# An attention and routed-experts kernel: weight chunks fetched one group later, one-hot rows and first split exchanged on GpSimd, the single-block scale on VectorE, a left-over half in front of a branch

## The chip, the cores and the metric

The kernel runs on one core of a Trainium2 chip. The metric is the time of one execution on the device in microseconds (us), lower is better. The engines of the core have a queue each and meet at semaphores: TensorE (PE; its weight loads are PEld), VectorE (DVE), ScalarE (ACT), GpSimd (POOL) and SyncE (SP), which issues most of the DMAs. A "q" behind an engine's name (ACTq) means its sequencer: branches, register loads and semaphore waits.

## The reference: what is computed

First attention over 4 batches of 8 heads, 768 positions of 64 numbers. Each query sees the keys less than 16 positions away, and 24 summaries, one for each block of 32 positions (the maximum of the keys, the mean of the values, with log 32 added to the score). The output, 3072 rows of 512 numbers, goes into a layer of eight experts with sticky routing:

```python
for s in range(S):
    fresh_e = int(np.argmax(logits[b, s]))
    if s == 0 or local_gate[b, s] < 0.5:
        e = fresh_e
    else:
        e = prev_e if prev_e >= 0 else fresh_e
    ...
    h = np.maximum(x[b, s] @ w1[e], 0.0)
    out[b, s] = p[e] * (h @ w2[e])
```

Here p is the softmax of the row's logits, w1 is 512 x 1024 and w2 is 1024 x 512 for each expert.

## The kernel before, in words

**Attention.** The 32 heads are 16 pairs (4 batches of 4 pairs), and each pair is done in two groups of 384 positions, so there are 32 groups, G = 0 to 31; pair n = G // 2. The loop over G in `attention` writes the instructions of all engines in one fixed order, and each engine runs its own in that order. In group G stand: `s_mm(G)`, the scores (L305 puts in the mask, L311 multiplies queries by the key windows kb); `t_stage(G - 2)`, transposes of the probabilities (L337, copied by ScalarE in L338); `s_max(G)` on VectorE (L319, the row maximum nm) and `s_exp(G)` on ScalarE (L327, six exponentials); `a_mm(G - 3)`, the value products (L348); `a_norm` on VectorE (L359, L360). Between them stand small steps of the routing of an earlier batch, which the method `small` lets in by counts of groups, and the transposes and logits of finished rows (L553, L570). One routing step, L640 on VectorE, writes sc, and the matmuls L644 to L647 on TensorE read it, in front of `a_mm(G - 3)` of group 26.

GpSimd prepares the next pair. In the first group of pair n come `windows(n + 1)` (L269, the keys' windows, scaled, into kb) and `fold_v(n + 1)` (L254, adds halves of the value blocks of vt into vf); in the second group `summaries(n + 1)` (L272, the block maxima ks, which VectorE computes in L243, into the last columns of kb) and `spread_v(n)` (L283, copies of the value means into vw). The scores of pair n + 1 cannot start before L272.

SyncE loads keys (kp, L197), queries (q, L206), values transposed (vt, L202) and value windows (vw, L210) some pairs ahead, and stores finished rows (L365), all through one queue.

**Jobs that ride along.** `tick(G, point)` runs jobs that were put at a group. Once the first batch is routed, the expert with the most rows of it, e0, is known, and `have_e0` places fetches and splits of e0's weights. A chunk is 128 x 1024 numbers, 512 KB: `wfetch` loads one into a buffer wst (four buffers, L1146), `wsplit` turns it into a high and a low part, ScalarE casting the high part (L1150), and GpSimd (four pieces, L1158) or VectorE (L1153) subtracting. The tables say at which G:

```python
SET0 = 25
WFETCH = (21, 21, 22, 22, 26, 30)
WSPLIT = (24, 29)
```

The same file has at point 1 of group SET0 the one-hot rows of the first batch, `self.set0()`: six GpSimd instructions (L682) that write A. In group G the order at the end is: GpSimd's windows and folds or summaries and copies, the loads, `tick(G, 1)`, `set0` if G is SET0.

**Experts.** Rows are sorted by expert into blocks of 128 and computed in calls of three, two or one blocks. `blocks` computes the first layer and all but one of the second-layer halves; the last half of each call is left to `left_over`, which runs in front of the next call and in which the next call's weights are split, under a branch that a flag (`words`) decides (`splits`, L1513). How many calls there are of each size depends on the data; every engine branches on a register: L1646 for calls of three, L1650 of two, L1662 of one. A single-block call is `single`: eight first-layer products in two halves, eight second-layer products, then `store`, which scales the result by the routing weight (psort) out of PSUM into yo, on ScalarE (L1205) where its third argument is true, on VectorE (L1208) otherwise, and scatters it to the output from GpSimd (L1209). After `store` the method loads two flags on ScalarE, VectorE and GpSimd and branches on them.

The end of the program reads so before:

```python
with tc.If(n1 > 0) as some:
    emit(self.left_over(AT1, splits(0, LANE3, 2), splits(1, LANE3)))
    call1(0)
    ...
with some.Else():
    emit(self.left_over(AT1))
```

With the data of these runs one call of one block is executed.

Of the kernel before, what the change touches and what calls it, by code (L numbers as in the profile page):

```python
# [35 lines left out]
CALL = 3  # L36
N3, N2, N1, MORE, SURE = 8, 8, 8, 2, 3
# [5 lines left out]
AT1 = AT2 + 2 + 2 * (N2 + MORE)  # L43
SLOTS = AT1 + 2 + N1 + MORE
LANE1, LANE2 = N3 + MORE, N3 + MORE + 1
LANE3 = LANE2 + N2 + MORE
# [4 lines left out]
WARM = 11  # L51
WHOLE = (3, 4, 5)
LATE = (*WHOLE, 9, 13)
SET0 = 25
BEHIND = (5, 16, 24, 30)
SOON = (8, 12)
FILL = {2: 5}

WFETCH = (21, 21, 22, 22, 26, 30)
WSPLIT = (24, 29)  # L60
WBY = "GGGVVVGV"

TAIL = {0: ("t", 30), 1: ("a", 29), 2: ("t", 31), 4: ("a", 30), 5: ("a", 31)}
# [21 lines left out]
class Kernel:  # L85
# [87 lines left out]
    def attention(self, tick, rows, tail):  # L173
        nc, tc, ident = self.nc, self.tc, self.ident
        with ExitStack() as ctx:
# [200 lines left out]
            for G in range(last_g):  # L376
# [84 lines left out]
                tick(G, 1)  # L461
                if G == SET0:
                    self.set0()
# [824 lines left out]
    def single(self, i, mid, w1, w2, refill):  # L1288

        nc = self.nc  # L1290
        hs = [self.mw.tile([P, 512], F32, name=f"hs{f}") for f in range(2)]

        def mm1(f, ks):
            for k in ks:
                if k == 0:
                    self.hp = self.bank("s")
                w = [x[0].rearrange("p (q k c) -> p q k c", k=KT, c=2 * P)[:, 2 * f:2 * f + 2, k] for x in (self.hi, self.lo)]
                self.mm(self.hp.rearrange("p (q c) -> p q c", q=2), self.xT[:, k, 0, 0], self.xT[:, k, 1, 0], w, k == 0, k == KT - 1)
                if k == KT - 1:
                    nc.scalar.activation(out=hs[f], in_=self.hp, func=AF.Relu)  # L1300

        mm1(0, range(KT))
        mm1(1, (0, 1))
        hT = [self.th(hs[0], 0), None]
        mm1(1, (2, 3))
        for w in range(2):
            refill(w, self.last_mm)
        yp = self.bank("a")

        def mm2(ks):  # L1310
            for k in ks:
                h, l = [x[:, P * (k % 4):P * (k % 4) + P] for x in hT[k // 4]]
                self.mm(yp, h, l, [x[1][:, k * DM:k * DM + DM] for x in (self.hi, self.lo)], k == 0, k == FT - 1)

        mm2((0, 1))
        hT[1] = self.th(hs[1], 1)
        mm2((2, 3))
        mid(0)
        mm2(range(4, 8))
        self.store(yp, i, True)  # L1320
        w1(0, 1, 2, 3)
        w2(0, 1, 2, 3)

# [53 lines left out]
    def run(self):  # L1377
        nc, tc = self.nc, self.tc
# [4 lines left out]
        def at(G, point, f, *args):  # L1383
            jobs.setdefault((G, point), []).append((f, args))
# [6 lines left out]
        def wfetch(j):  # L1391
            w, q = divmod(j, NCH)
            st["w", j] = self.awk.tile([P, CH], F32, name="wst", bufs=4)
            self.fetch(st["w", j], w, q * CH, (q + 1) * CH, st["e0"])

        def wsplit(j):
            w, q = divmod(j, NCH)
            self.split(w, q * CH, (q + 1) * CH, st.pop(("w", j)), nc.vector if WBY[j] == "V" else nc.gpsimd)

        def have_e0():  # L1400
            st["e0"] = nc.values_load(self.e0[0:1, 0:1], engines=(ENG.SP,), min_val=0, max_val=E - 1)
            for j in range(len(WSPLIT)):
                at(WSPLIT[j], 1, wsplit, j)
            for j in range(len(WFETCH)):
                at(WFETCH[j], 1, wfetch, j)

# [50 lines left out]
        def tail(stage):  # L1457
# [3 lines left out]
            for k in range(XL[-1] + 4):  # L1461
# [5 lines left out]
                if k in WLAST:  # L1467
                    wsplit(len(WSPLIT) + WLAST.index(k))
                if k in WLATE:
                    wfetch(len(WFETCH) + WLATE.index(k))  # L1470
                for u in range(NU):
# [8 lines left out]
        def reg(i, engines, hi):  # L1480
            return nc.values_load(self.words[0:1, i:i + 1], engines=engines, min_val=0, max_val=hi)  # L1481
# [7 lines left out]
        def split(w, chunks, by=None):  # L1489
            for q in chunks:  # L1490
                eng = nc.vector if SPLIT_BY[by or w][q] == "V" else nc.gpsimd
                self.split(w, q * CH, q * CH + CH, st["stage"][w][:, q * CH:q * CH + CH], eng)

        def have_all():
            while "words" not in st:
                self.small(1, True)

        def splits(w, lane, by=None):
            new = []

            def weights(*chunks):
                if lane is None:
                    return
                if lane == LANE1:
                    split(w, chunks)
                    if chunks[-1] == NCH - 1:
                        st["spent"].append(w)
                        refills()
                    return
                if not new:  # L1510
                    have_all()
                    new.append(reg(lane, (ENG.Activation, ENG.DVE, ENG.Pool), 1))
                with tc.If(new[0] > 0):  # L1513
                    split(w, chunks, by or (2 if w and lane else None))

            return weights

        def late(lane):
            r = []

            def weights(w, after):
                have_all()
                if not r:
                    r.extend((reg(2 * LANES + lane, (ENG.SP,), 1), reg(LANES + lane, (ENG.SP,), E - 1)))
                with tc.If(r[0] > 0):
                    refill(w, r[1], after)

            return weights

        def calls(n, blocks, lane):  # L1530

            def mid(half):
                if half < blocks:
                    while n < AT2 and st["next"] <= n + half:
                        self.small(1, True)
                    self.tx(n + half, half)
                    if n < AT2:
                        freed()
                    elif n + half + blocks < (AT1, SLOTS)[n >= AT1]:
                        self.gather(n + half + blocks)  # L1540

            return mid, splits(0, lane), splits(1, lane)
# [9 lines left out]
        with ExitStack() as ctx:  # L1552
# [10 lines left out]
            def refills():  # L1563
                if "words" in st:
                    while st["spent"]:
                        refill(st["spent"].pop(0), st["words"])
# [24 lines left out]
            def emit(*what):  # L1591
                for _ in chain(*what):
                    pass
# [51 lines left out]
            n3, n2, n1 = st["ends"]  # L1645
# [9 lines left out]
            def call1(n):  # L1655
                i = AT1 + 2 + n
                self.single(i, *calls(i + 1, 1, LANE3 + n + 1), late(LANE3 + n))

            with tc.If(n1 > 0) as some:
                emit(self.left_over(AT1, splits(0, LANE3, 2), splits(1, LANE3)))  # L1660
                call1(0)
                with ExitStack() as c:  # L1662
                    for n in range(1, N1):
                        c.enter_context(tc.If(n1 > CALL * n))
                        call1(n)
            with some.Else():
                emit(self.left_over(AT1))


def tile_kernel(tc, *args):  # L1670
# [90 lines left out]
```

## Time and profile before

| what | us |
|---|---|
| median of 3 runs | 436.49 |
| lowest and highest run | 434.3, 437.31 |
| the profiled execution | 433.81 |
| its span, first to last instruction | 432.0 |
| TensorE busy in the span | 416.2 |
| VectorE busy | 234.1 |
| ScalarE busy | 197.5 |
| GpSimd busy | 165.9 |

The profile is that of one execution. Start times count from the start of the span. A busy share is an average over stages that differ: attention fills the first 125 us or so, and the experts the rest. TensorE's matmuls are pipelined and their ends modelled, so a busy TensorE may still be one that waits a little; where it is listed with an idle time, it surely did.

### The profile page before, as it was taken

How to read it: one execution, taken by the hardware profiler on the slowest of the kernel's cores; microseconds unless marked ns; L12 is line 12 of the kernel's file. 1: busy time of each engine (PE TensorE's matmuls, PEld its weight loads, DVE VectorE, ACT ScalarE, POOL GpSimd, SP SyncE). 2: the span in 40 equal slices, each digit the busy share in tenths (PEclk: the TensorE clock that was granted, in tenths of full speed). 3: DMA queues.
4: the chain of work that ended last, by engine and by line, in shares of the span. 5: the costliest groups of instructions: out<-in, count | busy, mean ns of one | idle time of the engine just before them, and what ended most of it. 6: DMA issues, size and time to landing. Idle time of an engine off the chain costs nothing.

```text
span 432.0 us, 11296 instructions
## 1 busy us (share of the span) xinstructions
PE 416.2 (96%) x4227; PEld 360.3 (83%) x4228; DVE 234.1 (54%) x575; ACT 197.5 (46%) x466; POOL 165.9 (38%) x255
## 2 busy tenths in 40 slices
PE   7999999989999999999999999999999999999992
PEld 4787887868898798988987998799899889879781
DVE  4876796978788689957721022112435202254560
ACT  4988887967865227322121222122634212263561
POOL 3667686798624315753022103110630310321131
PEclk9999999989999999999999999999999999999997
DMA  8999999997251850394076912110257210219312
GB/s 310 403 396 402 400 329 377 401 402 284 95 177 68 325 212 0 99 368 170 2 284 231 374 52 72 29 50 0 99 185 255 90 58 0 57 53 388 105 51 58
DMA packets 22279, 83.27 MB, mean 193 GB/s; under 512 B 2702, under 2 KB 3344, under 8 KB 19120
## 3 DMA queue, kind: packets, MB, share of 16 engines
q1 hardware_dynamic: 17600, 67.75, 41.1%
q0 software_dynamic: 4448, 14.29, 10.0%
q8 instruction: 39, 0.64, 0.6%
q14 instruction: 48, 0.39, 0.3%
q10 hardware_dynamic: 144, 0.20, 0.2%
HBM read 69.65 MB, written 12.71 MB: 191 GB/s over the span
## 4 chain that ended last, share of the span: by engine, by line
issue 25%; DMA 12%; POOLq 5%; POOL 4%; PE 3%; DVE 3%; DVEq 0%
DMA out_dram<-yo,sidx 9%; POOLq L1273 4%; POOL xg L1164 2%; DMA out_dram<-few_y,sidx 2%; DMA xg<-x_dram,gidx 1%; DVE bp L1084 1%; POOL l L1158 1%; POOLq L1481 1%; PE bs L1249 1%; PE bt L1111 1%; PE bs L1251 0%; PE bs L1252 0%; DVE hT L1258 0%; DVE eqp L1078 0%; POOL out_dram L1209 0%
## 5 line engine op out<-in xcount | busy, mean ns | idle before, releaser
L1249 PE MATMUL bs<-xT,h 128*128 128x384 f32 (+1 forms) x288 | 91.3, 317 | 0.0
L1251 PE MATMUL bs<-xT,h 128*128 128x384 f32 (+1 forms) x288 | 89.8, 312 | 0.0
L1252 PE MATMUL bs<-xT,l 128*128 128x384 f32 (+1 forms) x288 | 89.7, 311 | 0.0
L1196 PE MATMUL ba<-h,hT 128*128 128x512 f32 x192 | 78.9, 411 | 1.4 <-PEq L1646 0.8
L1258 DVE SCALAR_TENSOR_TENSOR hT<-bs,hT 128x384 fp32r<-128x384 f32 (+1 forms) x56 | 33.2, 593 | 82.9 <-ACT hT L1256 69.2
L1198 PE MATMUL ba<-h,hT 128*128 128x512 f32 x192 | 75.3, 392 | 0.0
L1197 PE MATMUL ba<-l,hT 128*128 128x512 f32 x192 | 75.0, 391 | 0.0
L1256 ACT ACTIVATE hT<-bs 128x384 fp32r<-128x384 f32 (+1 forms) x56 | 29.3, 523 | 86.9 <-PE bs L1252 84.9
L1164 POOL DMA_INDIRECT xg<-x_dram,gidx x30 | 29.4, 981 | 101.5 <-PE bt L1175 90.5
L1249 PEld LDWEIGHTS bs<-xT,h 128*128 128x128 f32 x288 | 54.5, 189 | 0.8 <-issue 0.4
L327 ACT ACTIVATE pr<-bs,nm 128x120 f32<-128x120 f32 x192 | 51.7, 372 | 7.5 <-DVE nm L319 6.9
L1251 PEld LDWEIGHTS bs<-xT,h 128*128 128x128 f32 x288 | 54.5, 189 | 0.4
L1252 PEld LDWEIGHTS bs<-xT,l 128*128 128x128 f32 x288 | 54.5, 189 | 0.0
L1209 POOL DMA_INDIRECT out_dram<-yo,sidx x24 | 28.0, 1168 | 64.4 <-ACT yo L1205 40.9
L1196 PEld LDWEIGHTS ba<-h,hT 128*128 128x128 f32 x192 | 36.2, 189 | 8.7 <-issue 2.6
L1198 PEld LDWEIGHTS ba<-h,hT 128*128 128x128 f32 x192 | 36.0, 188 | 8.2
L1197 PEld LDWEIGHTS ba<-l,hT 128*128 128x128 f32 x192 | 36.2, 189 | 6.0
L1153 DVE TENSOR_TENSOR l<-stg,h 128x1024 fp32r<-128x1024 f32 x28 | 34.4, 1274 | 12.0 <-ACT h L1150 11.9
L1170 DVE TENSOR_TENSOR xT<-bt,xT 128x512 fp32r<-128x512 f32 x27 | 18.6, 691 | 36.5 <-ACT xT L1168 34.3
L1150 ACT CAST h<-stg 128x1024 fp32r<-128x1024 f32 x32 | 32.2, 1049 | 11.4 <-PEq L1646 4.6
L1205 ACT ACTIVATE yo<-ba,psort 128x512 f32<-128x512 f32 x24 | 16.5, 688 | 45.1 <-PE ba L1198 41.5
L283 POOL COPY vw<-vs 24x384 f32<-24x384 f32 x64 | 29.9, 509 | 13.6 <-ACT vs L278 5.4
(269 smaller groups left out, 639.4 us busy)
## 6 DMA issues: line engine op xcount, KB each, us to landing
stg<-in_w SPq DMA_DIRECT2D x16, 1024.0 KB, 7.7
vw<-in_vW SPq DMA_DIRECT2D x16, 780.0 KB, 7.4
few_w<-in_w SPq DMA_DIRECT2D x8, 1024.0 KB, 8.4
kp<-in_kT SPq DMA_DIRECT2D x16, 384.0 KB, 6.9
q<-in_qT SPq DMA_DIRECT2D x16, 384.0 KB, 7.6
vt<-in_vT SPq DMA_DIRECT2D x16, 384.0 KB, 7.0
x_dram<-xs SPq DMA_DIRECT2D x8, 768.0 KB, 5.8
wst<-in_w SPq DMA_DIRECT2D x8, 512.0 KB, 7.4
```

What stands on the lines that cost most here:

```text
L283: nc.gpsimd.tensor_copy(out=vw[n % 3][WL:W, t:t + NW // 4, :, 0:D], in_=vs.to_broadcast([NB, NW // 4, 2, D]))
L327: nc.scalar.activation(out=pr[:, h, u, 0:W], in_=sp[:, h, u, :], func=AF.Exp, bias=nm[:, h, u:u + 1], scale=1.0)
L1150: self.nc.scalar.copy(out=hi, in_=src)
L1153: eng.tensor_tensor(out=lo, in0=src, in1=hi.bitcast(F32), op=ALU.subtract)
L1164: self.nc.gpsimd.indirect_dma_start(out=t, out_offset=None, in_=rows, in_offset=bass.IndirectOffsetOnAxis(ap=self.gidx[:, i:i + 1], axis=0))
L1196: nc.tensor.matmul(out=ps, lhsT=ah, rhs=wh, start=first, stop=False)
L1197: nc.tensor.matmul(out=ps, lhsT=ah, rhs=wl, start=False, stop=False)
L1198: self.last_mm = nc.tensor.matmul(out=ps, lhsT=al, rhs=wh, start=False, stop=last).ins
L1249: ins = nc.tensor.matmul(out=ps[:, j], lhsT=wh, rhs=xh[c], start=(c == 0), stop=False).ins
L1251: nc.tensor.matmul(out=ps[:, j], lhsT=wh, rhs=xl[c], start=False, stop=False)
L1252: nc.tensor.matmul(out=ps[:, j], lhsT=wl, rhs=xh[c], start=False, stop=(c == KT - 1))
L1258: nc.vector.scalar_tensor_tensor(out=l, in0=ps, scalar=0.0, in1=h.bitcast(F32), op0=ALU.max, op1=ALU.subtract)
```

## The change

Five edits. The tables: the one-hot rows go from group 25 to group 24; the first four fetches of weight chunks from groups 21 and 22 to 22 and 23; the first split from group 24 to 25. In `single`, the store's scale goes from ScalarE to VectorE. At the end, `left_over` stands once, in front of the branch on n1, and the branch has no other side.

```diff
-SET0 = 25
+SET0 = 24
...
-WFETCH = (21, 21, 22, 22, 26, 30)
-WSPLIT = (24, 29)
+WFETCH = (22, 22, 23, 23, 26, 30)
+WSPLIT = (25, 29)
...
-        self.store(yp, i, True)
+        self.store(yp, i)
...
-            with tc.If(n1 > 0) as some:
-                emit(self.left_over(AT1, splits(0, LANE3, 2), splits(1, LANE3)))
-                call1(0)
-                with ExitStack() as c:
-                    for n in range(1, N1):
-                        c.enter_context(tc.If(n1 > CALL * n))
-                        call1(n)
-            with some.Else():
-                emit(self.left_over(AT1))
+            emit(self.left_over(AT1, splits(0, LANE3, 2), splits(1, LANE3)))
+            with ExitStack() as c:
+                for n in range(N1):
+                    c.enter_context(tc.If(n1 > CALL * n))
+                    call1(n)
```

On GpSimd, at the end of group 24 and through group 25 (l_122 and h_120 are the low and high parts of w1, wst a fetched chunk, A the one-hot rows, kb_139 the key windows of pair 13, vw_147 the value windows of pair 12):

```order
 L269 TENSOR_SCALAR kb_139<-kp_146 128x4x96 x3
 L254 TENSOR_TENSOR vf<-vt 128x192 x2
+L682 TENSOR_SCALAR A<-c_84,lanf 128x128 x6
+L272 TENSOR_SCALAR kb_139<-ks 128x12x24
+L283 COPY vw_147<-vs 24x6x64 x4
 L1158 TENSOR_TENSOR l_122<-wst,h_120 128x256 x4
-L272 TENSOR_SCALAR kb_139<-ks 128x12x24
-L283 COPY vw_147<-vs 24x6x64 x4
-L682 TENSOR_SCALAR A<-c_84,lanf 128x128 x6
 L269 TENSOR_SCALAR kb_138<-kp_145 128x4x96 x3
```

The split moves from in front of the summaries and copies to behind them, and the one-hot rows from behind the copies to in front of the summaries.

On SyncE, at the end of group 21 (kp_146 and q_136 are the keys and queries of pair 13, vt its values, vw_147 the value windows of pair 12; the ISA rows compute the address of a chunk):

```order
 L197 DMA kp_146<-in_kT 128x768
 L206 DMA q_136<-in_qT 128x768
-L1146 ISA
-L1146 DMA wst<-in_w 128x1024
-L1146 ISA
-L1146 DMA wst<-in_w 128x1024
 L202 DMA vt<-in_vT 128x768
 L210 DMA vw_147<-in_vW 128x1560
```

The first two chunks no longer stand in front of vt and vw; they come behind vw, and the next two behind the keys and queries of pair 14.

On VectorE, in the first single-block call (hT and xT are the low parts of transposed rows, yo the scaled result, words the flags):

```order
+L1660 COMPARE_AND_BRANCH
 L1170 TENSOR_TENSOR hT<-bt,hT 128x512
 L1525 UNCONDITIONAL_BRANCH x2
 L1170 TENSOR_TENSOR hT<-bt,hT 128x512
 L1170 TENSOR_TENSOR xT<-bt,xT 128x4x128
+L1208 TENSOR_SCALAR yo<-ba,psort 128x512
 L1481 TENSOR_LOAD words
 L1513 COMPARE_AND_BRANCH
```

The scale is new in VectorE's queue, in front of the loads of the flags; on ScalarE the same place loses L1205. The branch on n1, L1660 now, stands directly in front of the call.

## Rows read from the trace of the kernel before

**Rows 1.** Two stretches: busy us of each engine (instructions), granted clock, DMA share, GB/s.

```profile
92.05:95.46 3.41, 3.41 (x36) 3.00 (x34) 2.08 (x7) 2.81 (x9) 3.31 (x7) 0.51 1.02 397
95.55:104.15 8.60, 8.60 (x175) 7.35 (x178) 8.24 (x19) 6.73 (x23) 7.82 (x16) 1.00 0.90 334
```

**Rows 2.** Timeline of TensorE: start, duration, instruction, idle before it and what ended that.

```profile
88.25 0.35 PE L305 MATMUL bs<-me 64*64 64x360 bf16 x4
90.48 0.85 PE L311 MATMUL bs<-kb,q 64*64 64x120 f32 x24 [1.88 <-POOL kb L272]
91.26 0.87 PE L337 MATMUL bt<-ident,pr 128*124 128x128 f32 x6
91.96 0.17 PE L644 MATMUL bt<-sc,cb 128*128 128x8 bf16 x1
...
95.52 0.35 PE L305 MATMUL bs<-me 64*64 64x360 bf16 x4
...
99.15 0.35 PE L305 MATMUL bs<-me 64*64 64x360 bf16 x4
```

**Rows 3.** Timeline of GpSimd, groups 24 to 27.

```profile
84.85 1.15 POOL L254 TENSOR_TENSOR vf<-vt 128x192 f32<-128x192 f32 x2 [2.06 <-DMA vt<-in_vT]
87.25 2.78 POOL L1158 TENSOR_TENSOR l<-wst,h 128x256 fp32r<-128x256 f32 x4 [1.25 <-ACT h L1150]
89.99 0.43 POOL L272 TENSOR_SCALAR kb<-ks 128x288 f32<-128x288 f32 x1
90.49 1.85 POOL L283 COPY vw<-vs 24x384 f32<-24x384 f32 x4
92.44 3.52 POOL L682 TENSOR_SCALAR A<-c,lanf 128x128 bf16<-128x128 f32 x6
95.94 1.47 POOL L269 TENSOR_SCALAR kb<-kp 128x384 f32<-128x384 f32 x3
97.38 1.15 POOL L254 TENSOR_TENSOR vf<-vt 128x192 f32<-128x192 f32 x2
```

**Rows 4.** Timeline of VectorE in the same groups.

```profile
85.39 0.94 DVE L243 TENSOR_REDUCE ks<-kp 128x24 f32<-128x768 f32 x1
...
88.36 0.20 DVE L359 RECIPROCAL dn<-ba 128x6 f32<-128x6 f32 x1 [0.61 <-PE ba L348]
...
90.51 0.59 DVE L640 TENSOR_TENSOR_SCAN sc<-c,oh 128x48 bf16<-128x48 f32 x1
91.47 0.91 DVE L319 TENSOR_REDUCE nm<-bs 128x6 f32<-128x720 f32 x1 [0.37 <-PE bs L311]
...
93.78 0.20 DVE L359 RECIPROCAL dn<-ba 128x6 f32<-128x6 f32 x1 [1.29 <-PE ba L348]
...
97.45 1.50 DVE L664 TENSOR_SCALAR lb<-rho 128x6 int32<-128x6 int32 x1
```

**Rows 5.** Waits of SyncE: line, releaser, us in total, times, longest us.

```profile
SPq L1756 <- ACTq L1662: 1.3, 1, 1.3
```

**Rows 6.** Timeline of SyncE, DMA issues at the end of group 21.

```profile
75.79 0.89 SPq L1146 DMA_DIRECT2D wst<-in_w  x2
76.79 0.38 SPq L202 DMA_DIRECT2D vt<-in_vT  x1
```

**Rows 7.** Timeline of ScalarE: the first cast and the exponentials of group 25.

```profile
86.13 1.04 ACT L1150 CAST h<-wst 128x1024 fp32r<-128x1024 f32 x1
...
87.82 1.62 ACT L327 ACTIVATE pr<-bs,nm 128x120 f32<-128x120 f32 x6
```

**Rows 8.** Timeline of TensorE, the first matmul of the last left-over half.

```profile
406.10 0.49 PE L1196 MATMUL ba<-h,hT 128*128 128x512 f32 x1 [0.56 <-PEq L1650]
```

**Rows 9.** Timeline of the single-block call: last operations of VectorE and of ScalarE.

```profile
422.12 0.69 DVE L1170 TENSOR_TENSOR xT<-bt,xT 128x512 fp32r<-128x512 f32 x1 [1.17 <-ACT xT L1168]
...
424.27 0.69 ACT L1205 ACTIVATE yo<-ba,psort 128x512 f32<-128x512 f32 x1 [2.19 <-PE ba L1198]
```

**Rows 10.** Line 1662, the last branch: duration ns min/median/max, first and last start.

```profile
L1662 DVEq COMPARE_BRANCH  x2: 47/52/56, 423.6 to 426.7; - x2
...
L1662 ACTq EVENT_SEMAPHORE  x2: 17/17/17, 428.5 to 430.8; - x2
```

## The prediction

> **What bounds the kernel now.** I read three views in this order: the table of stages, the timeline of the stage that stands out, and the end of the program. In nearly all of the span TensorE runs without a gap at the full clock, so what can be won or lost lies where it does not. The first such place is around 88 to 96 us, late in attention. In the table the stretch from 92.05 us has a granted clock of 0.51, half of full speed (1.2 instead of 2.4 GHz), for 3.41 us, while the next stretch is at 1.00 [rows 1]. What TensorE did before the clock fell stands in its timeline: group 26 begins at 88.25 with its mask matmuls, and then the score matmuls wait 1.88 us for the summary columns that GpSimd (POOL) writes into kb; group 27 begins at 95.52 and group 28 at 99.15 [rows 2]. So group 26 took 7.27 us and group 27, with a similar load, 3.63.
>
> Why GpSimd was late is in its own rows: it idled 2.06 us for the values vt (until 84.85), then 1.25 us for ScalarE's cast of the first weight chunk, then spent 2.78 us on that chunk's split, and only then, at 89.99, wrote the summaries. The one-hot rows A, 3.52 us, for which all operands were long there, came last, at 92.44 [rows 3].
>
> The second bound is VectorE (DVE). From 95.55 to 104.15 it is busy 8.24 of 8.60 us [rows 1], so what TensorE wins at 88 us is only worth what VectorE can follow. Between 88.3 and 95.5 VectorE had two waits for TensorE of any size, 0.37 and 1.29 us [rows 4]. That cap is what I build on.
>
> The third place is the end. SyncE, which collects everything there, waits for the last scatter and after that 1.3 us more for ScalarE's sequencer (ACTq) [rows 5].
>
> **The change part by part.** *Fetches.* SyncE issued two chunks of weights (0.89 us) in front of vt [rows 6]; now vt goes first. The DMA share is 1.02 at 397 GB/s there [rows 1], so a queued transfer waits for the bytes ahead of it: two chunks are 1.05 MB, 2.6 us. GpSimd had vt at 84.85 and was free 2.06 us before, at 82.8; vt 2.6 us earlier is there at about 82.2, and the wait goes. The chunks land some 2 to 4 us later, about when the split, one group later, wants them; the total of bytes up to vt of the next pair is the same.
>
> *Rows and split exchanged.* New order on GpSimd: fold from 82.8 to 83.9 (1.15), A to 87.5 (3.52), summaries to 87.9 (0.43), copies to 89.8 (1.85), then the split. The column maxima ks that the summaries need end at 85.39 + 0.94 = 86.3 on VectorE [rows 4], so nothing new holds them. TensorE wants them at 90.48 - 1.88 = 88.6: the stall of 1.88 us goes, by a margin of 0.7, and with it what preceded the half clock.
>
> What is late next? Behind the summaries TensorE meets the routing matmuls L644 (91.96 before [rows 2]), which need sc from VectorE, and that chain did not wait for TensorE's stall: it starts with the normalisation at 88.36, after the value matmuls of the group before, and ends with L640 at 90.51 + 0.59 = 91.10 [rows 4]. So TensorE, with scores and transposes done 1.65 us after the scores begin (as from 90.48 to 91.26 + 0.87), near 90.2, waits about 0.9 us, half of the old stall. VectorE then goes on without its 0.37 and most of its 1.29, and from there it is the full engine. The gain in attention is therefore 0.37 + 1.29 = 1.66; I take 1.6. Bounds: 0, if the remaining wait is followed by the half clock all the same; and 7.27 - 3.63 = 3.6, all that TensorE lost, if VectorE's chain gets shorter too.
>
> The Trainium skill bears on that chain (SBUF — State Buffer, on the two separate sides of SBUF): GpSimd and VectorE share a port pair, an exclusive lock held for a whole instruction. By that rule an exchange on GpSimd also moves waits on VectorE, for better or worse; the row that agrees is L664, 1.50 us under GpSimd's fold and summaries. If the rule alone set the result, the second rival below would be the forecast.
>
> *The cast and split in their new place.* ScalarE's cast now follows the exponentials of group 25, which ended at 87.82 + 1.62 = 89.44 [rows 7] with a cast ahead of them, so it is done by 90.5 (1.04 more). Split to 93.3 (2.78), windows to 94.7 (1.47), fold to 95.9 (1.15), summaries of the next pair to 96.3. TensorE comes to group 28 at 99.15 - 1.6 = 97.5. Hidden, with 1.2 us to spare; if that cover is gone, it is the last rival.
>
> *Left-over half ahead of the branch.* The same instructions run, since one single-block call is executed here. TensorE loses one branch in a gap of 0.56 us [rows 8] and gets one later, behind queued matmuls. I take 0; it can be up to 0.5 either way, as the gap is a jump and its length hangs on where the code lies. The loads of the weight flags are unchanged.
>
> *Scale on VectorE.* The last store's scale took ScalarE 0.69 us; VectorE's nearest operation, a PSUM tile of the same size, took 0.69 as well [rows 9]. Equal, to within 0.1. What is queued behind it matters more: ScalarE sat 2.19 us in front of that scale [rows 9], and its exit (flag loads, a jump, semaphores, the last at 430.8 [rows 10]) could only follow. Now it leaves 2.2 us or more earlier, and VectorE takes the wait: from its last operation at 422.12 to its exit branch at 426.7 it needed 4.6 us [rows 9, 10], so from 424.27 it is out at 428.9, ahead of SyncE, which without ScalarE was 1.3 us from done when ScalarE came. The end is 1.3 us earlier, less 0.1 for the scale: 1.2. Bounds: 1.3 and -0.4 (the third rival).
>
> The Trainium skill (Runtime: NRT & Kernel Launch, on instruction fetch) says that a taken branch outside the fetched window forces a fetch before execution goes on. That speaks against this part, as where code lies now decides when an engine is out; the trace agrees in ScalarE's two exit semaphores, 2.3 us apart, where VectorE shows one gap only.
>
> **Sum.** 1.6 + 1.2 = 2.8 us off the profiled execution's 433.81 (span 432.0, 1.8 around it): 431.0. That execution lies 0.6% under the median of the runs, 436.49, whose own spread is 434.3 to 437.31; the same share, 0.65%, off the median gives 433.7.
>
> **Rivals.**
> 1. *VectorE's chain shortens as well.* For it: L664 took 1.50 us and the routing steps before L640 ran under the split; in the new order GpSimd idles where L664 comes. Against: other steps then meet the split and fold. All 3.6 us in attention: 436.49 - 4.8 = 431.7.
> 2. *The exit is fetched twice, now on VectorE.* ScalarE's second gap, 2.3 us, falls to VectorE: out at 428.9 + 2.3 = 431.2, 0.4 after ScalarE's 430.8. For it: such a gap is there on one engine of two. Against: the other engine had none. 436.49 - 1.6 + 0.4 = 435.3.
> 3. *Nothing won in attention.* TensorE's wait only changes its releaser, from GpSimd to VectorE, and the clock falls again. For it: 0.9 us of wait remain. Against: half of the old one. 436.49 - 1.2 = 435.3.
> 4. *Slower: the stall moves to group 28.* The split now stands in front of the next pair's windows, fold and summaries. If its chunk or cast is so late that these end 2 us after TensorE's arrival (99.5 instead of 96.3), the same pattern repeats: 1.9 us of stall and 3.41 us at half clock, 1.7 lost, where VectorE has no idle time to absorb it: 433.7 + 3.6 = 437.3. For it: GpSimd was busy nearly throughout. Against: 3.2 us of slack by my sum.
>
> **How the numbers follow.** Forecast 0.42, rival 1 0.22, rivals 2 and 3 0.14 each, rival 4 0.08. The likeliest gives 433.7. The range leaves out the upper tail of rival 4 and the lower one of rival 1, and takes in the spread of the runs: 430.0 to 436.4. About 1% (4.4 us) is what a measurement of this kernel can tell from no change: faster by more has most of rival 1 and a little of the forecast, 0.29; slower by more would need rival 4 and a bad run, 0.06; within it, 0.65.
>
> **What would show it.** Right: no wait of TensorE for kb near 88 us, a granted clock of 1.00 through 95 us, a wait of under 1.2 us at L644, group 28 some 1.6 us earlier; GpSimd in the order fold, A, summaries, copies, split without waiting for vt; at the end SyncE waiting last for the scatter, not for ScalarE. Wrong: the clock at half anywhere before the end, a wait for kb at group 28, SyncE waiting for VectorE's sequencer at the end, or group 28 at its old time though the stall is gone.

## The result and the profile after

The changed kernel took 431.37 us (median of 6 runs, 430.54 to 431.79), the kernel before 435.28 beside it (6 runs, 434.3 to 437.31): a ratio of 0.990, with a 95% interval of 0.9879 to 0.9921. That is 3.9 us, or 0.9 to 1.0%. The profiled execution after took 431.3 us with a span of 429.5, against 433.81 and 432.0 before. The forecast for that execution was 431.0, and for the median 433.7; the fall of the median is larger than that of the profiled execution, since the one profiled before was quicker than all six runs of its kernel listed here.

The table of two stretches, group 26 and groups 27 and 28 (start and end, length, then busy us and, in brackets, instructions of TensorE, its weight loads, VectorE, ScalarE, GpSimd; granted clock, DMA share, GB/s), for the kernel after:

```profile
88.48:93.05 4.57, 3.96 (x74) 3.14 (x71) 4.00 (x11) 4.10 (x14) 4.41 (x9) 1.00 1.02 391
93.05:101.71 8.66, 8.66 (x172) 7.41 (x171) 8.45 (x21) 7.49 (x26) 6.74 (x14) 1.00 1.04 408
```

The stretch at half speed of [rows 1] is gone: the granted clock is 1.00, which is 2.4 GHz. Group 26 takes 4.57 us where it took 7.27 [rows 2]. The two groups behind it take 8.66, as before (8.60 [rows 1]), and TensorE is busy all of that.

The timeline of TensorE after:

```profile
88.48 0.35 PE L305 MATMUL bs<-me 64*64 64x360 bf16 x4
88.74 0.84 PE L311 MATMUL bs<-kb,q 64*64 64x120 f32 x24
...
91.00 0.18 PE L644 MATMUL bt<-sc,cb 128*128 128x8 bf16 x1 [0.61 <-DVE sc L640]
...
93.05 0.35 PE L305 MATMUL bs<-me 64*64 64x360 bf16 x4
...
96.68 0.35 PE L305 MATMUL bs<-me 64*64 64x360 bf16 x4
```

The scores L311 no longer wait for kb (1.88 us in [rows 2]); in their place L644 waits 0.61 us for VectorE. Group 27 begins 2.47 us earlier than before, and so does group 28.

The timeline of GpSimd after, groups 24 to 27:

```profile
83.64 1.14 POOL L254 TENSOR_TENSOR vf<-vt 128x192 f32<-128x192 f32 x2 [0.95 <-DVE va L247]
84.77 3.51 POOL L682 TENSOR_SCALAR A<-c,lanf 128x128 bf16<-128x128 f32 x6
88.25 0.43 POOL L272 TENSOR_SCALAR kb<-ks 128x288 f32<-128x288 f32 x1
88.75 1.84 POOL L283 COPY vw<-vs 24x384 f32<-24x384 f32 x4
90.69 2.85 POOL L1158 TENSOR_TENSOR l<-wst,h 128x256 fp32r<-128x256 f32 x4
93.50 1.47 POOL L269 TENSOR_SCALAR kb<-kp 128x384 f32<-128x384 f32 x3
```

This is the new order, without the waits for vt and for the cast of [rows 3]. The fold waits 0.95 us for something else, VectorE's va, which is made from the buffer that the fold overwrites.

VectorE after:

```profile
88.59 0.20 DVE L359 RECIPROCAL dn<-ba 128x6 f32<-128x6 f32 x1 [0.18 <-PE ba L348]
...
89.30 0.41 DVE L629 TENSOR_TENSOR ev<-vm,carx 128x6 int32<-128x6 f32 x1
89.74 0.43 DVE L632 TENSOR_SCALAR e_all<-ev 128x6 int32<-128x6 int32 x1
90.21 0.44 DVE L635 TENSOR_TENSOR oh<-c,e_all 128x48 bf16<-128x48 f32 x1
90.68 0.26 DVE L640 TENSOR_TENSOR_SCAN sc<-c,oh 128x48 bf16<-128x48 f32 x1
...
92.14 0.20 DVE L359 RECIPROCAL dn<-ba 128x6 f32<-128x6 f32 x1 [0.29 <-PE ba L348]
...
95.30 0.26 DVE L664 TENSOR_SCALAR lb<-rho 128x6 int32<-128x6 int32 x1
```

Against [rows 4]: from the first reciprocal to the start of L664 it is 6.71 us, where it was 9.09. Of its waits for TensorE, 0.37, 1.29 and a third of 0.15 us for the scores of group 27, one of 0.29 is left; that is 1.5 of the 2.38 us. The rest, about 0.9, is for the most part shorter steps: L640 took 0.26 instead of 0.59 us.

The end after, first SyncE's waits, then the last scale:

```profile
SPq L1752 <- DMA out_dram<-yo,sidx: 20.4, 1, 20.4
...
SPq L1752 <- PEq L1752: 1.0, 2, 0.9
```

```profile
422.23 0.75 DVE L1208 TENSOR_SCALAR yo<-ba,psort 128x512 f32<-128x512 f32 x1 [1.42 <-PE ba L1198]
```

The wait for ScalarE [rows 5] is gone. The scale took 0.75 us on VectorE against 0.69 on ScalarE [rows 9]. From its start to the end of the span it is 7.27 us (422.23 to 429.5), before 7.73 (424.27 to 432.0): 0.46 us less, not 1.2.

### The profile page after: what moved, and what is told of

It is laid out like the page before. It is cut to its first block, busy times and chain, and to the rows that moved or that the text cites. A ratio compares the mean times of both kernels' runs of the same rounds, so it can differ in the third digit from the quotient of the medians.

```text
span 429.5 us, 11299 instructions
## 1 busy us (share of the span) xinstructions
PE 415.0 (97%) x4228; PEld 359.0 (84%) x4228; DVE 235.2 (55%) x576; ACT 196.6 (46%) x465; POOL 164.8 (38%) x255
## 4 chain that ended last, share of the span: by engine, by line
issue 24%; DMA 9%; PE 8%; POOLq 5%; POOL 4%; DVE 3%; ACT 0%; DVEq 0%
DMA out_dram<-yo,sidx 7%; POOLq L1273 4%; POOL xg L1164 2%; DMA xg<-x_dram,gidx 1%; PE ba L1196 1%; PE ba L1198 1%; PE ba L1197 1%; DVE bp L1084 1%; POOL l L1158 1%; PE bs L1249 1%; POOLq L1481 1%; PE bs L1252 1%; PE bs L1251 1%; PE bt L1111 1%; DMA out_dram<-few_y,sidx 1%
## 5 line engine op out<-in xcount | busy, mean ns | idle before, releaser
L1164 POOL DMA_INDIRECT xg<-x_dram,gidx x30 | 29.4, 979 | 100.9 <-PE bt L1175 90.1
L1205 ACT ACTIVATE yo<-ba,psort 128x512 f32<-128x512 f32 x23 | 15.8, 687 | 42.9 <-PE ba L1198 37.6
L283 POOL COPY vw<-vs 24x384 f32<-24x384 f32 x64 | 29.6, 503 | 13.9 <-ACT vs L278 5.0
```

The lines of the kernel that those rows point to most:

```text
L283: nc.gpsimd.tensor_copy(out=vw[n % 3][WL:W, t:t + NW // 4, :, 0:D], in_=vs.to_broadcast([NB, NW // 4, 2, D]))
L1164: self.nc.gpsimd.indirect_dma_start(out=t, out_offset=None, in_=rows, in_offset=bass.IndirectOffsetOnAxis(ap=self.gidx[:, i:i + 1], axis=0))
```

## The experiments

All times are medians of up to 12 runs beside runs of the kernel before on the same chip (434.9, 434.8, 434.83 and 436.13 us in the four sessions). Profiles of different executions are up to 1.6 us apart ahead of the stall (group 24 begins at 81.54 us in "rows25" and at 83.18 in "tables"), so stretches are compared, not start times.

**The parts alone.** Three kernels, each the kernel before with one part of the change; a fourth with the tables but for the fetches.

```diff
# tables
+SET0 = 24
+WFETCH = (22, 22, 23, 23, 26, 30)
+WSPLIT = (25, 29)
# scale
+        self.store(yp, i)
# branch
+            emit(self.left_over(AT1, splits(0, LANE3, 2), splits(1, LANE3)))
+            with ExitStack() as c:
...
# order_only
+SET0 = 24
+WSPLIT = (25, 29)
```

> Theory: the three tables alone carry most of the gain. No wait of TensorE for kb near 88 us, full clock through 95 us, group 27 begins 2 to 2.5 us earlier than before, 0.7 us of that is lost again by group 31, and the time is 1.7 to 3 us under the kernel before. Rival (the end carries it): under 1 us.

> Theory, from the trace of the changed kernel: SyncE no longer waits for ScalarE at the end, but of the 1.3 us of that wait only about 0.4 shows, because the scatter lands later and the last barrier is longer; 0.3 to 0.6 us faster. Rival A (the prediction's step): 1.2 us faster. Rival B (the exit fetched twice on VectorE): 0.4 us slower, SyncE waiting for DVEq.

> Theory: 0, to within 0.5 us; the two waits of TensorE for its sequencer at the branches, 0.82 and 0.56 us before, are 0.56 and 0.42 as in the changed kernel, so at most 0.4 us faster. Rival: code that lies elsewhere also changes the exit, and the end moves by 0.5 us or more.

> Rows and split exchanged (groups 24 and 25), the fetches left where they were, so vt still comes behind two chunks. Theory (the split in front of the summaries made the stall): GpSimd folds at 84.9 to 86.0, rows to 89.5, summaries at 89.9, so TensorE still waits for kb, about 1.3 us instead of 1.88, and the clock falls again: a gain under 1 us. Rival (the fetches hardly matter): no wait for kb over 0.3 us and the whole gain of the tables.

| kernel | median us | ratio to before, 95% interval |
|---|---|---|
| tables | 431.46 | 0.9931 (0.9911 to 0.9951) |
| scale | 434.13 | 0.9989 (0.9973 to 1.0005) |
| branch | 434.9 | 1.0004 (0.999 to 1.0018) |
| order_only | 433.5 | 0.9959 (0.9944 to 0.9973) |

The tables give 3.0 us (0.69% of 434.9), the scale 0.5 and the branch nothing; neither of the last two can be told from no change. The expected loss of 0.7 us by group 31 did not come with the tables alone: it belongs to the one profile of the changed kernel, where group 30 took 3.59 us instead of the 2.85 of "tables", with 0.30 us of idle TensorE for which the profile names no releaser. Group 26 in the table of stretches of "tables":

```profile
89.18:93.76 4.58, 3.96 (x74) 3.14 (x72) 4.01 (x11) 4.11 (x14) 4.43 (x9) 1.00 1.05 373
```

It is 4.58 us, as in the changed kernel. Not all of the 3.0 us lies in attention, though. From the start of group 21 to that of group 31 it is 38.07 us before and 35.30 with the tables, 2.8 less. The end is shorter too, though the tables change nothing there. The last matmul before, in "scale", in "tables" and in the changed kernel, whose spans end at 432.0, 431.1, 429.8 and 429.5:

```profile
423.80 0.39 PE L1198 MATMUL ba<-h,hT 128*128 128x512 f32 x1
```

```profile
423.59 0.39 PE L1198 MATMUL ba<-h,hT 128*128 128x512 f32 x1
```

```profile
422.44 0.39 PE L1198 MATMUL ba<-h,hT 128*128 128x512 f32 x1
```

```profile
421.81 0.39 PE L1198 MATMUL ba<-h,hT 128*128 128x512 f32 x1
```

From it to the end of the span it is 8.20 us before, 7.51 in "scale", 7.36 in "tables" and 7.69 in the changed kernel. With the order alone (TensorE, then GpSimd):

```profile
90.83 1.43 PE L311 MATMUL bs<-kb,q 64*64 64x120 f32 x24 [1.35 <-POOL kb L272]
```

```profile
85.71 1.15 POOL L254 TENSOR_TENSOR vf<-vt 128x192 f32<-128x192 f32 x2 [2.38 <-DVE nm L319]
```

The fold is late, and TensorE waits 1.35 us for kb, which is what was expected. (VectorE's nm is named as the releaser, but the fold reads no such tile; that the fold waits for vt, which still comes behind two chunks and landed at about 85.6 us, is the likely reason.) The gain of 1.8 us by the ratio (1.4 by the medians) is larger than the expected 1 us at most, and its profile cannot explain it: that execution was the slowest of the 12 (434.93 us) and took 0.5 us more than the kernel before from group 21 to group 31. The granted clock over the whole execution, 0.989 to 0.996 in its 12 runs where that of the kernel before was 0.985 to 0.994, would fit a fall that is less frequent or shorter after a shorter wait; that is not shown.

At the end, the last branch of "scale" and of "tables" (durations in ns, first and last start):

```profile
L1662 DVEq EVENT_SEMAPHORE  x2: 21/21/21, 428.8 to 428.9; - x2
```

```profile
L1662 ACTq EVENT_SEMAPHORE  x2: 17/17/17, 427.1 to 427.2; - x2
```

On VectorE the two exit semaphores stand 0.1 us apart: it has no second gap. But in "tables", where ScalarE still scales, ScalarE has none either, where before it had one of 2.3 us [rows 10]. In the seven kernels here whose last scale is on ScalarE, SyncE's wait for ScalarE at the end was 1.3 us (before), 1.0 (branch), 1.2 (order_only) and 0.6 (rows24_only, below), and not there in three (tables, fetch_only, rows25). The four with the wait have the old table of fetches, the three without it the new one. Each was traced once, so it stays open whether that table decides it or chance does.

From the last matmul to the end of the span it is 7.9 to 8.7 us in the four, 8.2 on average, 7.0 to 7.6 in the three, 7.3 on average, and 7.5 to 8.0 in the seven profiles with the scale on VectorE. Beside the old fetches the move of the scale therefore takes about 0.7 us from the end (8.2 to the 7.51 of "scale"), near the 0.5 of its median. Beside the new ones the profiles show no gain: 7.3 on average with ScalarE, 7.8 in the six with VectorE. That the whole 1.3 us did not show even beside the old ones has one visible reason: the last scatter landed 3.7 us after its issue in "scale", 3.2 before.

**Why the tables work.** Four more kernels: only the fetches; the new fetches and split with the rows left at 25; only the rows; and the changed kernel again.

```diff
# fetch_only
+WFETCH = (22, 22, 23, 23, 26, 30)
# rows25
+WFETCH = (22, 22, 23, 23, 26, 30)
+WSPLIT = (25, 29)
# rows24_only
+SET0 = 24
```

> The first four fetches one group later, split and rows where they were. Theory (the fetch only matters together with the exchange): vt lands 2.7 us earlier, at 82.0, the first chunk 2.8 later, at 85.2, still before its cast at 86.1, so the split ends near 90 as before and the wait of TensorE for kb is again 1.5 to 2 us, the clock falls, and the time is that of the kernel before to within 0.7 us. Rival (the late vt made the stall): the wait falls under 0.5 us and the time by 2 us or more.

> The changed tables, but the one-hot rows left at group 25, so that they follow the split. Theory: summaries at 87 and no wait for kb near 88, but GpSimd reaches the split at 89.3, waits about 1.2 us for the cast (ScalarE, behind the exponentials), splits to 93.4, writes the rows to 96.9, and the next pair's windows, fold and summaries end near 100.5, where TensorE comes to group 28 at 96.7: a new wait of 3 us there and a fall of the clock; the time is that of the kernel before, to within 1.5 us. Rival (the place of the rows does not matter once the split is behind the summaries): as fast as with all three tables, 431.5.

> Only the one-hot rows one group earlier; they then stand in front of the summaries and behind the split. Theory: summaries 3.5 us later, at 93.5, so TensorE waits 5.4 us for kb instead of 1.88; group 27 begins 3.5 us later, the half clock follows, and of those 3.5 us nothing is won back, since GpSimd no longer holds anything behind it: 3 to 4 us slower. Rival (VectorE hides part of it): 1 to 2 us slower.

> The changed kernel once more beside its parts. Theory: the parts add up, tables 3.4 us, scale 0.7, branch 0, to 4.1 us under the kernel before, within 0.5. Rival (they overlap): 3.4 us or less.

| kernel | median us | ratio to before, 95% interval |
|---|---|---|
| fetch_only | 434.2 | 0.9984 (0.9965 to 1.0003) |
| rows25 | 436.31 | 1.0037 (1.0018 to 1.0056) |
| rows24_only | 439.03 | 1.0099 (1.0071 to 1.0126) |
| all_again | 431.82 | 0.9926 (0.9898 to 0.9954) |

For "fetch_only" and "rows25" the theory held on the time, at its edges (0.6 us faster where up to 0.7 was allowed, 1.5 slower where up to 1.5 was), for "rows24_only" nearly (4.2 us slower, not 3 to 4). For "all_again" the sum of 4.1 us was too high, as it was made from differences of medians and single profiles; by the ratios the parts give 3.0 + 0.5 - 0.2 = 3.3, and 3.2 was measured.

"fetch_only" was expected to lose its full clock after a wait of 1.5 to 2 us. It waited 2.40, did not lose the clock in its profile, and met a second wait at group 28 as well. What it gained does not lie in attention, where its profile took 39.41 us from group 21 to group 31, 1.3 more than before; its end was 7.02 us, 1.2 less. It shows what the clock costs (TensorE, then stretches):

```profile
91.49 0.84 PE L311 MATMUL bs<-kb,q 64*64 64x120 f32 x24 [2.40 <-POOL kb L272]
...
100.72 0.85 PE L311 MATMUL bs<-kb,q 64*64 64x120 f32 x24 [1.73 <-POOL kb L272]
```

```profile
88.75:95.02 6.27, 3.87 (x73) 3.19 (x70) 4.44 (x11) 3.82 (x15) 6.11 (x12) 1.00 1.02 382
```

In this execution the clock did not fall after either wait. Group 26 takes 6.27 us, of which 2.40 are the wait: 3.87 for its work, where the kernel before needed 7.27 - 1.88 = 5.39. So the stretch at half speed cost 1.5 us, and the wait of 1.88 less the 0.61 that stays at L644 1.3: together 2.8, about the 2.7 us by which group 26 became shorter.

"rows25" gives both sides of the exchange. GpSimd, TensorE and the clock at group 28:

```profile
89.59 2.79 POOL L1158 TENSOR_TENSOR l<-wst,h 128x256 fp32r<-128x256 f32 x4 [1.21 <-issue]
92.36 3.52 POOL L682 TENSOR_SCALAR A<-c,lanf 128x128 bf16<-128x128 f32 x6
...
99.09 0.42 POOL L272 TENSOR_SCALAR kb<-ks 128x288 f32<-128x288 f32 x1
```

```profile
99.57 1.48 PE L311 MATMUL bs<-kb,q 64*64 64x120 f32 x24 [4.22 <-POOL kb L272]
```

```profile
99.50:102.80 3.30, 3.23 (x48) 2.44 (x48) 1.42 (x5) 0.00 (x0) 3.15 (x8) 0.50 1.02 418
```

GpSimd stands idle 1.21 us in front of the split, does the rows behind it, and the next pair's summaries come at 99.09; TensorE waits 4.22 us and then runs at half speed. That is the forecast's last rival, and it makes the time 4.9 us longer than with the rows in front (436.31 to 431.46). The rows are the filler that covers the chunk's flight and its cast.

The same profile has group 26 in 3.86 us (87.41 to 91.27 on TensorE), without a wait at L644. VectorE's steps in front of L644:

```profile
88.21 0.19 DVE L629 TENSOR_TENSOR ev<-vm,carx 128x6 int32<-128x6 f32 x1
88.44 0.17 DVE L632 TENSOR_SCALAR e_all<-ev 128x6 int32<-128x6 int32 x1
88.64 0.21 DVE L635 TENSOR_TENSOR oh<-c,e_all 128x48 bf16<-128x48 f32 x1
88.88 0.26 DVE L640 TENSOR_TENSOR_SCAN sc<-c,oh 128x48 bf16<-128x48 f32 x1
```

They take 0.93 us from the first start to the last end, beside a GpSimd that stands idle from 88.4 to 89.59; in the changed kernel, beside the copies L283, 1.64 (89.30 to 90.94). A busy GpSimd is not enough for long steps, however. In "order_only" the first two ran beside the rows L682 (86.84 to 90.36) and were as short:

```profile
89.95 0.19 DVE L629 TENSOR_TENSOR ev<-vm,carx 128x6 int32<-128x6 f32 x1
90.18 0.21 DVE L632 TENSOR_SCALAR e_all<-ev 128x6 int32<-128x6 int32 x1
```

The next two, beside the summaries and the copies, took 0.40 and 0.58 us there.

The Trainium skill (SBUF — State Buffer, on the two separate sides of SBUF) has GpSimd and certain operations of VectorE share a port pair under an exclusive lock. The traces agree with it in part: steps are longer beside the copies, not beside the rows, and L664 took 1.50 us beside the fold L254 before and 0.26 beside the same operation after. What sets the length of a step stays open.

"rows24_only" has the longest wait, and the price of it:

```profile
94.42 1.48 PE L311 MATMUL bs<-kb,q 64*64 64x120 f32 x24 [5.77 <-POOL kb L272]
```

```profile
88.29:100.30 12.01, 6.24 (x71) 5.28 (x69) 4.98 (x11) 4.40 (x16) 10.49 (x20) 0.72 0.71 280
```

Group 26 takes 12.01 us instead of 7.27, 4.7 longer for a wait that is 3.9 longer, and the kernel 4.2 more (439.03 to 434.8). VectorE hides nothing.

**What is late next.** "all_again" is the changed kernel, 3.0 us under the kernel before, but its profiled execution took 433.9 us. The place is another one (TensorE, GpSimd, stretches):

```profile
111.68 1.01 PE L1175 MATMUL bt<-ident,xg 128*128 128x128 f32 x4 [1.68 <-DMA xg<-x_dram,gidx]
```

```profile
103.65 1.15 POOL L254 TENSOR_TENSOR vf<-vt 128x192 f32<-128x192 f32 x2 [2.29 <-DMA vt<-in_vT]
...
105.36 1.18 POOL L1164 DMA_INDIRECT xg<-x_dram,gidx  x1 [0.17 <-DVE tl L860]
```

```profile
111.70:114.90 3.20, 3.20 (x32) 2.75 (x33) 1.32 (x3) 0.59 (x1) 2.70 (x6) 0.51 0.39 137
```

TensorE comes to the transposes of the first gathered rows xg before they have landed, waits 1.68 us, and the clock stands at half for at least 3.2 us. The gathers stand behind the last fold in GpSimd's queue, and that fold waits 2.29 us for vt. Two attempts to move the transfers, and one to use the idle GpSimd, on top of the changed kernel:

```diff
# fetch30
+WFETCH = (22, 22, 23, 23, 30, 30)
# rows23_fetch30
+SET0 = 23
+WFETCH = (22, 22, 23, 23, 30, 30)
# fetch_late
+WFETCH = (22, 27, 29, 29, 30, 30)
```

> The changed kernel with the fifth chunk fetched at group 30 instead of 26. Theory (what is late next are the transfers): without its 512 KB in the queue at 95 us the value windows and the gathered rows xg land about 1.3 us earlier, the wait of TensorE for xg near 110 us (1.68 us and a fall of the clock in one profile of the changed kernel, 0.30 and none in two others) does not appear, and the runs are those of the changed kernel without its slower ones: 0.3 to 1 us faster than it. Rival (the gathers are held by GpSimd, not by the transfers): no difference.

> The same, and the one-hot rows at group 23, in front of the windows of pair 13. Theory (VectorE's small steps take twice as long while GpSimd works): GpSimd reaches the split about 0.9 us before the cast is done, so the steps in front of L644 run partly beside an idle GpSimd and the wait of 0.62 us at L644 falls to 0.1 to 0.4: 0.2 to 0.5 us faster than with the fifth chunk alone. Rival (an earlier stretch of VectorE is hit instead, under the rows at 81 to 85 us, and group 24 or 25 becomes longer by as much): no gain or a loss up to 0.5 us.

> The changed kernel beside the two above. Theory: 431.5 within 0.5 us as before, some of its runs with a wait for xg near 110 us and a time above 432. Rival (that wait was an accident of one execution): no wait over 0.5 us there and a time of 431.0.

> The changed kernel with the second chunk fetched at group 27 and the others at 29 and 30: 1.5 MB fewer stand in the queue in front of vt of the last pair. Theory (from the last three profiles: vt of the last pair lands at 102 to 103.5 us because the transfers are busy throughout, GpSimd waits about 2 us for it, the gathers of xg stand behind it in GpSimd's queue, and TensorE, now 2.5 us earlier, sometimes comes to xg too early and then loses 1.7 us of wait and 1.7 us of clock): vt lands about 3 us earlier, GpSimd does not wait for it, no wait for xg, and the runs of 433 us and more do not appear: 430.5 to 431.2, 0.3 to 1 us under the changed kernel. Rival (the queue in front of vt does not set when the rows land): slower runs remain, 431.5.

| kernel | median us | ratio to before, 95% interval | lowest, highest run |
|---|---|---|---|
| fetch30 | 431.52 | 0.9943 (0.992 to 0.9965) | 430.77, 434.96 |
| rows23_fetch30 | 432.14 | 0.9948 (0.992 to 0.9975) | 429.6, 435.93 |
| all_third (the changed kernel) | 431.31 | 0.9929 (0.9911 to 0.9947) | 430.79, 431.96 |
| fetch_late (before: 436.13) | 432.63 | 0.9927 (0.9913 to 0.9941) | 432.23, 433.0 |

"fetch30" missed: the wait is still there.

```profile
110.90 1.09 PE L1175 MATMUL bt<-ident,xg 128*128 128x128 f32 x4 [1.67 <-DMA xg<-x_dram,gidx]
```

The fifth chunk is issued behind vt (in the changed kernel at 94.80, vt at 93.43), and without it the fold still waited 2.25 us for vt. "rows23_fetch30" shortened the wait at L644 as expected,

```profile
90.66 0.18 PE L644 MATMUL bt<-sc,cb 128*128 128x8 bf16 x1 [0.17 <-DVE sc L640]
```

and group 26 with it, from 4.57 to 3.99 us (88.72 to 92.71), but the time did not follow: its median is not lower and its runs spread over 6 us. What that spread comes from was not traced. "fetch_late" took the chunks out from in front of vt (GpSimd, TensorE):

```profile
100.64 1.15 POOL L254 TENSOR_TENSOR vf<-vt 128x192 f32<-128x192 f32 x2
...
103.16 1.18 POOL L1164 DMA_INDIRECT xg<-x_dram,gidx  x1 [0.38 <-DVE gidx L857]
```

```profile
111.40 0.63 PE L1175 MATMUL bt<-ident,xg 128*128 128x128 f32 x4 [0.23 <-DMA xg<-x_dram,gidx]
```

Here the theory was half right. GpSimd no longer waits for vt, and the gathers are issued at 103.16 instead of 105.36 (all_again); but three chunks are now fetched next to them, and TensorE still meets xg with a wait of 0.23 us. None of its 6 runs is 0.5 us over their median, yet the ratio is that of the changed kernel. "all_third" shows no wait for xg at all, so the 1.68 us comes in some executions only. The fold's wait for vt does not decide it: in "all_third" it is 2.28 us, and its two gathers are issued at 104.59 and 106.07, in "fetch30" at 104.58 and 106.06. The rows of the second were there without a wait, with all transposes of xg done by 110.2, in the one, and came at 110.9 in the other. So the flight of the gather differs, and what lengthens it was not traced. The 12 runs of "fetch30" fall into seven of 430.8 to 431.9 us and five of 433.1 to 435.0, and the one with the wait (433.46) is of the second kind. Of the versions tried, none is faster than the changed kernel beyond the intervals.

## Why the prediction was right, and where its terms were off

**The sign and the size** were right: 431.0 forecast for the profiled execution, 431.3 measured; 433.7 for the median, inside the range of 430.0 to 436.4, with 431.37 measured, further down than the likeliest case. Of these 2.3 us 1.2 lie in the base: 436.49 was the median of three runs, and with three more it is 435.28. Rival 1's 431.7 lies nearer, but its terms, 3.6 and 1.2, are not what the parts gave either. The three comparisons of the changed kernel give 0.990, 0.9926 and 0.9929. The sum of 2.8 us is near the measured 3.0 to 3.9, but its terms are not: attention was too small and the end too large, and it is luck that the two errors nearly cancel. (Twice the prediction counts its rivals one too far: what the rule of the port pair would bring is rival 1, and the bound of -0.4 is rival 2.)

**Attention, 1.6 forecast, 2.8 measured** (from group 21 to group 31 in the profile of the tables alone; their whole time gives 3.0, with 0.9 us to either side, of which the profile has 0.8 at the end). The changed kernel's own profiles have 1.5, 3.1 and 2.9; that the first of them is near the forecast is luck, as it lost 0.8 us again behind group 26. The mechanism is as told: the stall at kb gone, the half clock gone, L644 next with 0.61 us (0.9 forecast). The step that failed is the cap: "VectorE then goes on without its 0.37 and most of its 1.29, and from there it is the full engine. The gain in attention is therefore 0.37 + 1.29 = 1.66". That took VectorE's steps to be as long as before. They were not, and its path to L664 became 2.38 us shorter, of which waits were 1.5. So TensorE won back most of what it had lost: the 7.27 us of group 26 became 4.57, against 3.63 at the upper bound. That is what rival 1 said of VectorE's chain; it went too far in the size, since 0.61 us of wait remain.

**Fetches.** vt was forecast at 82.2, and the wait for it is gone. The fold began at 83.64, not 82.8, because of va, a wait on VectorE that had been hidden behind the one for vt. The fetch alone brings 0.7 us (0.8 either way, so it can be nothing, and its profile has it at the end and not in attention), the order alone 1.8, both together 3.0 by the ratio and 3.4 by the medians: order_only left 1.35 us of wait for kb, and fetch_only 2.40.

**Rows, split and group 28.** Summaries were forecast to end at 87.9 and ended at 88.68, just as TensorE began the scores at 88.74: the margin of 0.7 was used up by va. The split ended at 93.5 (93.3 forecast). That the rows cover the flight of the chunk was not said in the prediction; "rows25" shows it. The last rival did not come, but the margin was small: the next pair's summaries were done at 96.49 us (96.3 forecast), and TensorE, earlier than forecast, began the scores of group 28 at 96.85, so 0.4 us were left of the 1.2 to spare. Its forecast price of 3.6 us was of the right order: 4.9 in "rows25", where it came.

**Branch, 0 forecast**: 1.0004 with 0.999 to 1.0018. Right.

**The end, 1.2 forecast, 0.5 measured** (interval 1.2 to -0.2). VectorE's way out took 4.9 us from the scale (422.23 to 427.1; 4.6 forecast), and no second gap came: rival 2 fell. The step that failed is "The end is 1.3 us earlier": it took the 1.3 us of one profile for what the change would win. That wait was not there in any of the three profiles with the new fetches and the scale still on ScalarE, so in the changed kernel the new fetches may have removed it before the scale did; and beside the old fetches about 0.7 us of the end were won. The interval alone would still admit the 1.2; the profiles of the end speak against it.

The Trainium skill (Runtime: NRT & Kernel Launch, on instruction fetch) lets a taken branch outside the fetched window cost a fetch. The traces agree that there are gaps at the exit: the same instructions on ScalarE show one of 2.3 us in the profile of the kernel before and none in that of "tables". That these gaps are fetches, and what makes them come and go, no run here shows.

**Rival 3**, nothing won in attention, fell with the granted clock of 1.00 in the row of group 26.

## What to carry to other kernels

A stall is worth more than its wait when the clock falls behind it: here 1.3 us of wait carried 1.5 us of half clock with it, and half of the gain. Before an engine next to the stall is taken as the cap, ask which of its steps ran beside the work that is moved, since they need not keep their length. When a job is moved out from in front of a needed result, look for a job that can stand in the hole in front of it: the exchange without the rows was slower than no exchange. And a wait that is read off a single profile, above all one at the end that depends on a jump, should be looked up in a second profile, and in one with the other parts of the change, before its full length enters a sum.

## What was not expected of the hardware

- Waits of like length are not always followed by the half clock: after 2.40 us for kb the granted clock stayed at 1.00 in "fetch_only", and after 2.40 us it fell in "scale" (0.66 over the 5.04 us from 90.27 to 95.31); after 1.88 us it was 0.51 for 3.41 us in the kernel before, and after 1.35 us in "order_only" it was 0.51 for 3.37 us.
- The same four VectorE steps took 0.93 us beside a GpSimd that was idle for most of it, 1.64 us beside copies and, before, 2.03 us (89.07 to 91.10) beside the split, the summaries and copies; beside the one-hot rows two of them were as short as beside an idle GpSimd.
- Transfers need not follow when TensorE gets ahead: the last vt was issued at 95.1 us before and landed 5.8 us later, at 100.9; in "all_third" it was issued at 93.3 and landed 9.5 us later, at 102.8. The DMA share in that stretch of the changed kernel was 1.04 at 408 GB/s.
